# The spatial product of a gMLP block as seven products of quarters, in two passes

## The chip, the cores and the metric

One Trainium2 chip, one core. The time is device microseconds of one execution, the median of the runs; smaller is better. Next to the runs there is one execution under the hardware profiler, whose trace gives all durations used here.

## The reference

An attention block and a gMLP block follow each other on x of 2048 x 512, each after a LayerNorm. The change lies in the second:

```
h   = x + attention(layernorm(x))            # 32 heads of 16
z   = gelu(layernorm(h) @ w_in)              # 2048 x 1376, split into z1 and z of 688 columns each
z2  = layernorm(z[:, 688:])
g   = w_sp @ z2 + b_sp[:, None]              # w_sp is 2048 x 2048
out = h + (z1 * g) @ w_out                   # w_out is 688 x 512
```

## The kernel before

A row block is 128 rows, so there are 16. Matrix products are made in fp32r from two parts of each operand: a high part, rounded by a copy (ScalarE or GpSimd), and a low part, the difference (VectorE or GpSimd). `split` (line 73) makes both; `mm3` (83) issues three matmuls, high x high, high x low and low x high, into one PSUM bank.

The program has four stages: projections (243 to 527), attention (575 to 702), the z stage (719 to 769) and the gate stage (772 to 835). In the first two the order on TensorE, ScalarE, VectorE and the SP queue is written out by hand (`manual_schedule`); in the last two a scheduler orders each engine's instructions by its own estimate of times. Every engine executes its list strictly in order, and so does a DMA queue: SP issues all DMAs of these stages, in the order of its list, each after its waits.

In the z stage `load_o` (542 on) fetches a row block of the attention's output and the reciprocals of the softmax sums, and GpSimd multiplies them; `split_o` makes the parts. `make_h` (560 on) is the output projection (12 matmuls of 512 columns), the residual and the LayerNorm `hn`, whose mean, reciprocal root (`rstd_of`, ten small VectorE operations) and scaling (573) are VectorE's. `turn` (724) transposes `hn` into the parts `hT`. `make_z` (733) multiplies by w_in (48 matmuls of 344 columns), takes gelu on ScalarE, stores z1 to DRAM by SP's queue, normalises z2 on VectorE (752) and keeps both parts of it in SBUF for all 16 blocks; GpSimd makes the low part. Blocks go from 0 to 15. In one turn of the loop stand the projection of block sb+2, the transposes of sb+1 and the z matmuls of sb. The first two `make_h` lie in the last units of the attention stage. The last `invert` (620) of the attention stage takes the reciprocal of the softmax sums, which come by a DMA; its VectorE operation (624) falls into the beginning of the z stage.

In the gate stage `load_ws` (709) fetches one row block of w_sp (transposed on input, 1 MB) and splits it, one block ahead. `gate` (789) makes two PSUM banks of 344 columns, 16 x 3 matmuls each, adds the bias and multiplies by z1 on VectorE (803). `finish` (807), one block behind, transposes the product (six pieces in one PSUM tile, `pr` into `pT`), multiplies it by w_out (18 matmuls of 512 columns), adds h and stores. `load_wu` splits w_out on GpSimd.

Of the kernel before, what the change touches and what calls it, by code (L numbers as in the profile page):

```python
# [18 lines left out]
P = 128  # L19
# [5 lines left out]
EPS = 1e-5  # L25
GUESS = float(0x5F3759DF - (1 << 22) - (1 << 31))
NB = S // P
NQ = S // 512
DB = D // P
HG = H // 4  # L30
# [13 lines left out]
def block_kernel(ctx: ExitStack, tc: tile.TileContext, x, wqkv, wo, w_in, w_sp4, b_sp, w_out, out):  # L44
# [26 lines left out]
    z_scr = dram.tile([S, FH], F32, name="z_scr")  # L71

    def split(hi, lo, src, eh=None, el=None):

# [452 lines left out]
        m = LEAD  # L527


    wc = ctx.enter_context(tc.tile_pool(name="wc", bufs=3))  # L530
    early = ctx.enter_context(ExitStack())
    ec = early.enter_context(tc.tile_pool(name="early_c", bufs=1))
    e2 = early.enter_context(tc.tile_pool(name="early_2", bufs=2))
    wo2 = [wc.tile([P, DB, D], F32R, name=f"wo{i}", tag="w8") for i in range(2)]
# [24 lines left out]
    def make_h(sb, acc):  # L559
# [12 lines left out]
        hns[sb] = e2.tile([P, D], F32, name="hn")  # L572
        nc.vector.tensor_scalar(hns[sb], h, mv[:, 0:1], rs, op0=ALU.subtract, op1=ALU.mult)

    with ExitStack() as at:
        kpool1 = at.enter_context(tc.tile_pool(name="kpool1", bufs=1))
# [51 lines left out]

        def load_weights(i):

            t = wc.tile([P, DB * D], F32, name="wg", tag="w8")
# [14 lines left out]
        with tc.manual_schedule(engines={E.PE, E.Activation, E.DVE, E.SP}):  # L646
            for n in range(0, len(units), 2):
# [43 lines left out]
                if n % 32 == 16 and n < 6 * 32:  # L691
                    load_weights(n // 32)
                if n in (498, 502, 506):
                    load_o((n - 498) // 4)
                if n in (502, 506):
                    split_o((n - 502) // 4)
                if n in (504, 508):
                    make_h((n - 504) // 4, later[0].tile([P, 512], F32, name="h"))
# [7 lines left out]
    z2 = [zc.tile([P, NB, FH], F32R, name=f"z2{i}") for i in range(2)]  # L706
    wsp = [wc]

    def load_ws(tb):
        pool = wsp[tb % 2]  # L710
        t = pool.tile([P, NB, P], F32, name="wt", tag="w8")
        nc.sync.dma_start(t, w_sp4[tb])
        ws = [pool.tile([P, NB, P], F32R, name=f"ws{i}", tag="w8") for i in range(2)]
        for k in range(2):
            b = slice(k * NB // 2, (k + 1) * NB // 2)
            split(ws[0][:, b, :], ws[1][:, b, :], t[:, b, :], "act")
        return ws

    with ExitStack() as mid:
        m2 = mid.enter_context(tc.tile_pool(name="mid_2", bufs=2))  # L720
        ps = mid.enter_context(tc.tile_pool(name="mid_ps", bufs=5, space=PSUM))
        pt = mid.enter_context(tc.tile_pool(name="mid_pt", bufs=2, space=PSUM))

# [8 lines left out]

        def make_z(sb):
            hT = hTs.pop(sb)
            z = [m2.tile([P, FH], F32, name=f"z{i}") for i in range(2)]
            st = m2.tile([P, 2, 6], F32, name="zst")
            for i in (1, 0):
                for c in range(2):
# [17 lines left out]
        turn(0)  # L756
        split_o(2)
        for sb in range(NB):
            if sb + 2 < NB:
                make_h(sb + 2, ps.tile([P, 512], F32, name="acc"))  # L760
            if sb + 3 < NB:
                load_o(sb + 3)
                split_o(sb + 3)
            if sb + 1 < NB:
                turn(sb + 1)
            if sb == NB - 2:
                ws = load_ws(0)
            make_z(sb)
    early.close()


    with ExitStack() as fin:
        fc_ = fin.enter_context(tc.tile_pool(name="fin_c", bufs=1))
        f2 = fin.enter_context(tc.tile_pool(name="fin_2", bufs=2))
        wsp.append(fin.enter_context(tc.tile_pool(name="fin_w", bufs=3)))
# [3 lines left out]
        wu = [fc_.tile([P, len(FB), D], F32R, name=f"wu{i}") for i in range(2)]  # L779

        def load_wu():
            t = f2.tile([P, len(FB), D], F32, name="wg", bufs=1)
            nb, fn = len(FB) - 1, FB[-1][1]
            nc.sync.dma_start(t[:, :nb, :], w_out[:nb * P, :].rearrange("(a p) c -> p a c", p=P))
            nc.sync.dma_start(t[:fn, nb, :], w_out[nb * P:, :])
            for i, (_, n) in enumerate(FB):
                split(wu[0][:n, i, :], wu[1][:n, i, :], t[:n, i, :], "pool", "pool")

        def gate(tb, ws):

            rows = slice(tb * P, (tb + 1) * P)
            z1 = f2.tile([P, FH], F32, name="z1")
            nc.sync.dma_start(z1, z_scr[rows, :])
            g = [ps_g.tile([P, 512], F32, name="g") for i in range(2)]
            for i in range(2):
                f = slice(i * FC, (i + 1) * FC)
                for sb in range(NB):
                    mm3(g[i][:, :FC], ws[0][:, sb, :], ws[1][:, sb, :],
                        z2[0][:, sb, f], z2[1][:, sb, f], sb == 0, sb == NB - 1)
            pr = f2.tile([P, FH], F32, name="pr")  # L800
            for i in range(2):
                f = slice(i * FC, (i + 1) * FC)
                nc.vector.scalar_tensor_tensor(pr[:, f], g[i][:, :FC], bias[:, tb:tb + 1], z1[:, f],  # L803
                                               op0=ALU.add, op1=ALU.mult)
            return pr

        def finish(tb, pr):
            rows = slice(tb * P, (tb + 1) * P)
            h = f2.tile([P, D], F32, name="h")
            nc.sync.dma_start(h, h_scr[rows, :])  # L810
            pT = [f2.tile([P, len(FB), P], F32R, name=f"pT{i}") for i in range(2)]
            tp = ps_t.tile([P, 8, P], F32, name="tp")
            for i, (f0, fn) in enumerate(FB):
                nc.tensor.transpose(tp[:fn, i, :], pr[:, f0:f0 + fn], ident)  # L814
                if i in (1, 4, 5):
                    b = slice({1: 0, 4: 2, 5: 5}[i], i + 1)
                    split(pT[0][:fn, b, :], pT[1][:fn, b, :], tp[:fn, b, :], "act")
            acc = ps_o.tile([P, 512], F32, name="acc")
            for i, (f0, fn) in enumerate(FB):
                mm3(acc, pT[0][:fn, i, :], pT[1][:fn, i, :],  # L820
                    wu[0][:fn, i, :], wu[1][:fn, i, :], i == 0, i == len(FB) - 1)
            y = f2.tile([P, D], F32, name="y")
            nc.vector.tensor_add(y, acc, h)
            nc.sync.dma_start(out[rows, :], y)

        prev = None
        for tb in range(NB):
            nxt = load_ws(tb + 1) if tb + 1 < NB else None
            if tb == 0:
                load_wu()  # L830
            pr = gate(tb, ws)
            if prev is not None:
                finish(tb - 1, prev)
            prev, ws = pr, nxt
        finish(NB - 1, prev)


# [27 lines left out]
```

## Time and profile before

| | us |
|---|---|
| median of 3 runs (1926.92 to 1932.78) | 1927.6 |
| the profiled execution | 1930.47 |
| its span (first to last instruction) | 1928.7 |
| projections, attention: 0 to 1421.58 | 1421.6 |
| z stage: 1421.58 to 1594.68 | 173.1 |
| gate stage: 1594.68 to the end | 334.0 |

| engine | busy us | share of the span |
|---|---|---|
| TensorE (PE) | 1911.9 | 99% |
| VectorE (DVE) | 1444.7 | 75% |
| ScalarE (ACT) | 1261.6 | 65% |
| GpSimd (POOL) | 139.7 | 7% |

The mean granted TensorE clock is 0.998 of full speed. A row of a group gives its line, engine, operation, tiles, shapes and count, then busy time in us and mean duration in ns, then the idle time of the engine just before such instructions and what ended it. A line of the time line gives start and duration in us, the instruction, and in brackets the idle time before it and its releaser. Matmuls overlap in the array: the duration is the latency of one, and the distance between two starts is what it costs.

### The profile page before, as it was taken

The page shows a single profiled execution, that of the slowest core. Times are in us where ns is not written, and L with a number is a line of the kernel's source. Part 1 is how long each engine was busy: PE and PEld are TensorE (multiplying, and loading weights), DVE is VectorE, ACT ScalarE, POOL GpSimd, SP SyncE. Part 2 cuts the span into 40 slices and gives each one's busy share as a digit, 9 for nine tenths or more (in the row PEclk, how much of TensorE's full clock was granted, in tenths as well). Part 3 has the DMA queues.
Part 4 walks back from the last instruction along what each step waited for, and adds up shares of the span by engine and source line. Part 5 has one row for each costly group of instructions (what it writes and reads, how often), then busy time and mean ns, then how long its engine had stood idle before and what let it go on. Part 6 is the DMA issues. An engine that isn't in the chain of part 4 may idle for free.

```text
span 1928.7 us, 31977 instructions
## 1 busy us (share of the span) xinstructions
PE 1911.9 (99%) x11800; PEld 1094.2 (57%) x11800; DVE 1444.7 (75%) x2886; ACT 1261.6 (65%) x1590; POOL 139.7 (7%) x201
## 2 busy tenths in 40 slices
PE   9999999999999999999999999999999999999999
PEld 6765444444444344444444444444369999989987
DVE  6487999999999999999999999999358773232231
ACT  3335888888888888888888888888943331111110
POOL 2130000101011000000000000000012222000000
PEclk9999999999999999999999999999999999999999
DMA  5777111211221120111021021000143334232210
GB/s 187 194 190 175 40 24 32 71 24 28 50 53 49 38 40 22 31 37 24 24 53 24 13 51 37 13 13 6 29 118 118 109 119 175 81 109 92 81 66 34
DMA packets 121845, 128.90 MB, mean 67 GB/s; under 512 B 60248, under 2 KB 80744, under 8 KB 118104
## 3 DMA queue, kind: packets, MB, share of 16 engines
q1 hardware_dynamic: 121656, 126.84, 24.4%
q8 instruction: 93, 1.52, 0.3%
q14 instruction: 64, 0.52, 0.1%
q0 software_dynamic: 32, 0.01, 0.0%
HBM read 84.32 MB, written 41.55 MB: 65 GB/s over the span
## 4 chain that ended last, share of the span: by engine, by line
PE 93%; DVE 2%; DMA 1%; ACT 1%; SPq 1%; issue 1%; POOL 0%; ACTq 0%; POOLq 0%; DVEq 0%
PE pv L604 25%; PE m L200 25%; PE s L593 12%; PE acc L84 6%; PE acc L86 5%; PE acc L85 5%; PE g L85 4%; PE g L84 4%; PE g L86 4%; PE tp L814 1%; ACT pt L596 0%; DMA rc<-r_scr 0%; DVE rs_t L101 0%; DMA xr<-in_x 0%; SPq L547 0%
## 5 line engine op out<-in xcount | busy, mean ns | idle before, releaser
L596 ACT ACTIVATE pt<-s 128x1024 f32<-128x1024 f32 x1024 | 993.2, 1030 | 144.5 <-PE s L593 140.5
L205 DVE TENSOR_REDUCE mx<-m 128x1 f32<-128x512 f32 x1511 | 958.7, 684 | 105.2 <-PE m L200 64.7
L200 PE MATMUL m<-kst,qst 48*128 48x512 f32 x1511 | 607.1, 448 | 0.0
L604 PE MATMUL pv<-pt,vst 128*32 128x512 f32 x4096 | 550.7, 605 | 0.4 <-ACT o L611 0.4
L593 PE MATMUL s<-qst,kst 50*128 50x512 f32 x2048 | 465.6, 428 | 2.6 <-ACT pt L596 2.0
L200 PEld LDWEIGHTS m<-kst,qst 48*128 48x128 f32 x1511 | 263.2, 184 | 315.8 <-DVE mx L205 221.7
L593 PEld LDWEIGHTS s<-qst,kst 50*128 50x128 f32 x2048 | 223.2, 185 | 56.8 <-ACT pt L596 32.4
L200 PE MATMUL m<-uvs,qst 48*128 48x512 f32 x503 | 249.0, 496 | 0.0
L200 PEld LDWEIGHTS m<-uvs,qst 48*128 48x128 f32 x503 | 91.8, 183 | 207.3 <-DVE mx L205 205.3
L214 DVE CUSTOM_DVE_ANT_0 ab<-m,ab 128x512 f32<-128x512 f32 x252 | 171.6, 681 | 3.7 <-ACT ab L210 2.0
L604 PEld LDWEIGHTS pv<-pt,vst 128*32 128x32 f32 x4096 | 82.9, 108 | 160.9 <-issue 155.1
L76 ACT ACTIVATE ws<-wt 128x1024 fp32r<-128x1024 f32 x32 | 33.6, 1055 | 210.8 <-PE g L85 203.6
L84 PE MATMUL g<-z,ws 128*128 128x344 f32 x512 | 165.2, 323 | 0.6 <-issue 0.6
L85 PE MATMUL g<-z,ws 128*128 128x344 f32 x512 | 164.7, 322 | 0.0
L86 PE MATMUL g<-z,ws 128*128 128x344 f32 x512 | 163.4, 319 | 0.0
L210 ACT ACTIVATE ab<-m 128x512 f32<-128x512 f32 x251 | 151.0, 602 | 16.7 <-PE m L200 16.3
L803 DVE SCALAR_TENSOR_TENSOR pr<-g,bias,z 128x344 f32<-128x344 f32 x32 | 18.4, 576 | 182.3 <-PE g L86 180.3
L85 PEld LDWEIGHTS g<-z,ws 128*128 128x128 f32 x512 | 96.2, 188 | 5.8 <-issue 5.2
L84 PEld LDWEIGHTS g<-z,ws 128*128 128x128 f32 x512 | 96.2, 188 | 0.9 <-issue 0.9
L86 PEld LDWEIGHTS g<-z,ws 128*128 128x128 f32 x512 | 96.2, 188 | 0.6
L84 PE MATMUL acc<-wi,hT 128*128 128x344 f32 x256 | 83.7, 327 | 0.0
L86 PE MATMUL acc<-wi,hT 128*128 128x344 f32 x256 | 82.4, 322 | 0.0
(136 smaller groups left out, 1603.7 us busy)
## 6 DMA issues: line engine op xcount, KB each, us to landing
wt<-in_w_sp SPq DMA_DIRECT2D x16, 1024.0 KB
qst<-q_scr SPq DMA_DIRECT2D x192, 64.0 KB
kst<-k_scr SPq DMA_DIRECT2D x48, 256.0 KB
k_scr<-part SPq DMA_DIRECT2D x16, 512.0 KB
q_scr<-part SPq DMA_DIRECT2D x16, 512.0 KB
z_scr<-z SPq DMA_DIRECT2D x16, 344.0 KB
z<-z_scr SPq DMA_DIRECT2D x16, 344.0 KB
xg<-in_x SPq DMA_DIRECT2D x16, 256.0 KB
```

The costliest lines, as they stand in the source:

```text
L76: nc.scalar.activation(hi, src, AF.Copy)
L84: nc.tensor.matmul(ps, lh, rh, start=first, stop=False)
L85: nc.tensor.matmul(ps, lh, rl, start=False, stop=False)
L86: nc.tensor.matmul(ps, ll, rh, start=False, stop=last)
L200: nc.tensor.matmul(acc, q[r, p, c], keys[r, p], start=True, stop=True)
L205: nc.vector.reduce_max(at(t, e if t else e - 1), acc, axis=AX.X)
L210: nc.scalar.activation(ab[0], acc, AF.Abs)
L214: nc.vector.tensor_tensor_reduce(ab[0], acc, ab[0], 0.5, LOW, ALU.add, ALU.max, at(0, 0))
L593: nc.tensor.matmul(s[:, t, :], k[r, p, kb * P:(kb + 1) * P], q[r, p, :], start=True, stop=True)
L596: nc.scalar.activation(t, s, AF.Exp, scale=DH ** -0.5)
L604: nc.tensor.matmul(pv[0][32 * j:32 * j + 32, :], vst[hg % 2][:, c:c + 32], pts[j % 2][:, j // 2, :], start=kb == 0, stop=kb == NB - 1)
L814: nc.tensor.transpose(tp[:fn, i, :], pr[:, f0:f0 + fn], ident)
```

## The change

The four quarters of w_sp (A11 to A22, 1024 x 1024) and of z2 (B11 to B22, 1024 x 344) give the four quarters of the result by seven products, one eighth of the matmuls less, with sums of quarters ahead of and behind the products. HB is 8; p numbers a pair of row blocks, p and p+8.

- z stage: z rows run in the order 0, 8, 1, 9, ...; h rows in 0, 1, 8, 9, 2, 10, .... Both normalisations are made by ScalarE from a factor and an offset (`normal`), except for the two h in the attention stage. z1 and the normalised z2 are stored by ScalarE's queue. After each second block GpSimd makes four sums of that pair's quarters and both parts of each (`T`); for the last pair VectorE and ScalarE do.
- Pass 1 (scheduled): for each p four products, with A11-A21, (A21+A22)-A11, A22 and A21+A22 as left operands, made by VectorE from halves of rows loaded by SP (256 KB each). The second sum is stored in `s_scr`; three partial results go to `g_scr`. B11 is loaded back and split, one block per p. In the last p the loads for pass 2 (B22, B21, w_out) begin, in the buffers that pass 1 frees.
- Pass 2 (`manual_schedule` for TensorE, ScalarE and VectorE): for each p the products A11 x B11, S4 x B22, A12 x B21, the multiplication by z1 (mostly GpSimd) and the output of both row blocks, with the transposes of one block between the halves of a product.

```diff
+    z_rows = [sb + HB * i for sb in range(HB) for i in range(2)]
+    h_rows = [0, 1, HB, HB + 1] + z_rows[4:]
...
+    def normal(out, z, mv, rs, pool):
+
+        nb = pool.tile([P, 1], F32, name="nb")
+        nc.vector.tensor_scalar(nb, rs, mv[:, 0:1], -1.0, op0=ALU.mult, op1=ALU.mult)
+        nc.scalar.activation(out, z, AF.Identity, bias=nb, scale=rs)
...
+    def rows_of_a(p, e):
...
+        load_a(a11, 0, 0, p)
+        load_a(a21, 1, 0, p)
+        load_a(a22, 1, 1, p)
+        combine(e, s3, a11, a21, ALU.subtract)
+        combine(e, a21, a21, a22, ALU.add)
+        combine(e, a11, a21, a11, ALU.subtract)
+        for n in range(2):
+            nc.sync.dma_start(cut(s_scr[p])[n], a11[n])
+        return {"s3": s3, "s2": a11, "a22": a22, "s1": a21}
...
-            nc.sync.dma_start(z_scr[sb * P:(sb + 1) * P, :], z[0])
+            nc.scalar.dma_start(z_scr[0][rows, :], z[0])
...
-            rs = rstd_of(m2, mv[:, 1:2], 1)
-            nc.vector.tensor_scalar(z[1], z[1], mv[:, 0:1], rs, op0=ALU.subtract, op1=ALU.mult)
-            split(z2[0][:, sb, :], z2[1][:, sb, :], z[1],
-                  "act" if sb < NB - 1 else None, "pool" if sb < NB - 2 else None)
+            normal(z[1], z[1], mv, rstd_of(m2, mv[:, 1:2], 1), m2)
+            nc.scalar.dma_start(z_scr[1][rows, :], z[1])
...
+            e = nc.gpsimd if el else nc.vector
...
+            e.tensor_sub(b11, b12, b11)
+            e.tensor_sub(b12, b22, b12)
+            e.tensor_sub(t2, b22, b11)
+            put_t("t3", b12)
+            put_t("t2", t2)
+            put_t("t1", b11)
+            e.tensor_sub(b11, b21, t2)
+            put_t("n4", b11)
...
+        for k in range(NB):
+            if k + 2 < NB:
+                make_h(h_rows[k + 2], ps.tile([P, 512], F32, name="acc"))
...
+            if k + 1 < NB:
+                turn(z_rows[k + 1])
+            make_z(z_rows[k])
+            if k == NB - 2:
+                raw = rows_of_a(0, nc.vector)
+                ops = {n: put(w[i], raw[n]) for i, n in enumerate(("s3", "s2", "a22"))}
...
+        for p in range(HB):
...
+            load_b(b11, 0, 0, p)
+            if p:
+                product(g7, ops["s3"], T["t3"])
+            else:
+                for blocks in (range(HB - 1), range(HB - 1, HB)):
+                    product(g7, ops["s3"], T["t3"], blocks)
+                    product(g6, ops["s2"], T["t2"], blocks)
...
+                b22 = [zc.tile([P, HB, FC], F32R, name="b22", tag=f"t3_{i}") for i in range(2)]
+                for k in range(HB):
+                    load_b(b22, 1, 1, k)
...
+            nc.scalar.activation(p6, g6, AF.Copy)
+            nc.vector.tensor_add(p67, g7, p6)
...
+            product(g4, ops["a22"], T["n4"])
+            keep(1, g4, p67)
...
+            product(g5, ops["s1"], T["t1"])
+            keep(2, g5, p67)
+            keep(0, g5, p6)
...
+                product(g1, a11, b11, halves[0])
+                if prev:
+                    prev.turn((0, 2), (2, 5), (5, 6))
+                product(g1, a11, b11, halves[1])
...
+                (nc.gpsimd if p else nc.vector).tensor_mul(bot.pr, bot.pr, z1[1])
...
+                if prev:
+                    prev.multiply(range(len(FB)))
+                product(g3, s4, b22, halves[0])
...
+                bot.turn((0, 2), (2, 5), (5, 6))
+                product(g3, s4, b22, halves[1])
+                nc.vector.tensor_add(right, g3, right)
+                nc.gpsimd.tensor_mul(right, right, z1[0][:, FC:])
...
+                bot.multiply(range(len(FB)))
+                product(g2, a12, b21, halves[0])
+                bot.store()
...
+                product(g2, a12, b21, halves[1])
+                nc.vector.tensor_add(left, g2, left)
+                (nc.vector if last else nc.gpsimd).tensor_mul(left, left, z1[0][:, :FC])
```

More of the change, by code (lines that the diff above doesn't have):

```diff
@@ new lines, in load_a, with cut, put, combine @@
+    def load_a(halves, i, j, p):
+        for n, t in enumerate(halves):
+            nc.sync.dma_start(t, w_sp4[p + HB * i][:, HB * j + QB * n:HB * j + QB * n + QB, :])
+    def cut(t):
+        return [t[:, QB * n:QB * n + QB, :] for n in range(2)]
+    def put(slot, halves):
+        op = slot.take()
+        for n in range(2):
+            parts(cut(op[0])[n], cut(op[1])[n], halves[n])
+        return op
+    def combine(e, out, a, b, op):
+        for n in range(2):
+            e.tensor_tensor(out[n], a[n], b[n], op)
@@ L756, in block_kernel @@
[L756 to L768, printed above, removed]
+            normal(z[1], z[1], mv, rstd_of(m2, mv[:, 1:2], 1), m2)
+            nc.scalar.dma_start(z_scr[1][rows, :], z[1])
@@ L789, in gate @@
[L789 to L794, printed above, removed]
-            for i in range(2):
[L796 to L835, printed above, removed]
+        b11 = [bc.tile([P, HB, FC], F32R, name=f"b11_{i}") for i in range(2)]
+        def load_b(b, i, j, k):
+            t = f1.tile([P, FC], F32, name="b", bufs=3)
+            nc.sync.dma_start(t, z_scr[1][(HB * i + k) * P:(HB * i + k + 1) * P, j * FC:(j + 1) * FC])
+            parts(b[0][:, k, :], b[1][:, k, :], t)
@@ new lines, in product, with load_wu @@
+        def product(acc, a, b, blocks=range(HB)):
+            for k in blocks:
+                mm3(acc, a[0][:, k, :], a[1][:, k, :], b[0][:, k, :], b[1][:, k, :],
+                    k == 0, k == HB - 1)
+        def load_wu(i, hi, lo):
+            f0, fn = FB[i]
+            t = e2.tile([P, D], F32, name="wu", tag="hn", bufs=3)
+            nc.sync.dma_start(t[:fn], w_out[f0:f0 + fn, :])
+            parts(hi, lo, t[:fn], "pool")
+        f = [Slot(fs, f"f{i}") for i in range(3)]
+        ops["s1"] = put(f[0], raw["s1"])
@@ new lines, in block_kernel, with __init__, turn, multiply @@
+        class Out:
+            def __init__(self, tb, h, pr):
+                self.rows, self.h, self.pr = slice(tb * P, (tb + 1) * P), h, pr
+                self.pT = self.acc = None
+            def turn(self, *groups):
+                if self.pT is None:
+                    self.pT = [f2.tile([P, len(FB), P], F32R, name=f"pT{i}") for i in range(2)]
+                    self.tp = ps_t.tile([P, 8, P], F32, name="tp")
+                for i0, i1 in groups:
+                    fn = FB[i1 - 1][1]
+                    for i in range(i0, i1):
+                        f0, n = FB[i]
+                        nc.tensor.transpose(self.tp[:n, i, :], self.pr[:, f0:f0 + n], ident)
+                    split(self.pT[0][:fn, i0:i1, :], self.pT[1][:fn, i0:i1, :],
+                          self.tp[:fn, i0:i1, :], "act")
+            def multiply(self, blocks, end=True):
+                first = self.acc is None
+                if first:
+                    self.acc = ps_o.tile([P, 512], F32, name="acc")
+                for i in blocks:
+                    n = FB[i][1]
+                    mm3(self.acc, self.pT[0][:n, i, :], self.pT[1][:n, i, :], wu[0][i], wu[1][i],
+                        first and i == blocks[0], end and i == blocks[-1])
+            def store(self):
+                y = f2.tile([P, D], F32, name="y")
+                nc.vector.tensor_add(y, self.acc, self.h)
+                nc.sync.dma_start(out[self.rows, :], y)
```

187 lines of the change are left out of this document (153 added, 34 removed).

## The prediction

> **What bounds the kernel now.** I read the busy time by stage first, then the matmul pitch in the time line of the last stage, then what TensorE waited for around the two stage borders, and last the costs of the engines that get new work. Busy time by stage (columns: window, length, busy time of each engine with its instructions, granted clock, DMA share, GB/s); the two lines are the z stage (lines 719 to 768) and the gate stage (772 to 835):
>
> ```profile
> core 0: us, PE busy (x) PEld busy (x) DVE busy (x) ACT busy (x) POOL busy (x), PEclk, DMA share, GB/s
> 1421.58:1594.68 173.10, 169.26 (x1003) 159.93 (x1001) 134.44 (x395) 57.66 (x112) 39.48 (x26) 0.99 0.38 115
> 1594.68:1928.70 334.02, 329.17 (x1920) 300.33 (x1920) 87.19 (x128) 47.04 (x78) 12.89 (x12) 1.00 0.27 92
> ```
>
> TensorE fills both. In the gate stage VectorE is busy 26% of the time and ScalarE 14%, so matmuls taken out there are time taken out until another resource is full. The time line gives what one costs, and the groups by line what follows it:
>
> ```profile
> 1644.27 0.32 PE L85 MATMUL g<-z,ws 128*128 128x344 f32 x1
> ...
> 1645.36 0.32 PE L86 MATMUL g<-z,ws 128*128 128x344 f32 x1
> ...
> L803 DVE SCALAR_TENSOR_TENSOR pr<-g,bias,z 128x344 f32<-128x344 f32 x32 | 18.4, 576 | 182.3 <-PE g L86 180.3
> ```
>
> The starts run from 1644.27 to 1645.36 in seven steps: 0.156 us per 344-column matmul (0.32 is its latency). A row block takes 20.57 us (chain: 1632.45 to 1653.05, 20.60), of which 96 x 0.156 = 15.0 is the gate and 5.57 the transposes and 18 output matmuls (pitch 0.233, 4.2 us).
>
> **What goes.** A pair of row blocks (p, p+8) had 2 x 96 = 192 gate matmuls; seven quarter products of 8 blocks x 3 are 168. So 24 x 0.156 = 3.74 us per pair, times 8: 30.0 us. The written order also sets each block's transposes in one run between two half products, where 1645.5 to 1653.0 now changes six times between transposes, output and gate matmuls. 5.57 us hold 4.2 of output matmuls and 0.8 of six transposes (four take 0.57 in the z stage); of the 0.57 left I take 0.13 a block off, 2 us in all (bounds 0 and 9). Gain 32 us, if the products are fed.
>
> **What the feeding costs in the steady blocks.** Pass 1, 15.0 us of TensorE per p. VectorE: 6 sums and 8 low parts of 128x512 at half of the 1.2 us that a 128x1024 subtraction takes alone (1626.05), 14 x 0.61 = 8.5, four adds out of PSUM at about 0.5 (three products are kept and p67), a low part of B11 0.45: 11 us, 73%. ScalarE: 8 copies of 128x512 at 0.62 and two of 344 at 0.46, 5.9 us. Both are under 15, and the operands of p+1 are made during p, six slots for four operands, so nothing of it is late. Pass 2, 22 us per p: 3 x 0.58, 8 x 0.61, six pT low parts 2.5, two y 1.4, two adds 1.0: 11.5 us on VectorE. The one short path is g2 to the next p's transposes: add 0.5, GpSimd's multiply (688 columns take 1.74, so 344 take 0.87), hops 0.2: 1.6 us against a half product of 12 x 0.156 = 1.87. Bounds 0 and 0.7 us for each of seven p; I take 0.15, 1 us.
>
> The z stage keeps its matmuls. VectorE gives the two normalisations to ScalarE (0.61 and 0.79 a block) and gets two 128x1 factors (0.2 each). ScalarE gets 1.4 us and two DMA issues (0.3 to 0.7 each on SP) to about 3.4 us of 10.8. GpSimd had 1.74 + 1.29 a block:
>
> ```profile
> L81 POOL TENSOR_TENSOR z<-z,z 128x688 fp32r<-128x688 f32 x14 | 24.4, 1742 | 24.3 <-ACT z L76 22.3 <-PE acc L86 2.0
> L78 POOL CAST wqk<-wg 128x512 fp32r<-128x512 f32 x6 | 3.7, 614 | 38.9 <-DMA wg<-in_wqkv 38.9
> L81 DVE TENSOR_TENSOR o<-o,o 128x512 fp32r<-128x512 f32 x13 | 17.8, 1367 | 11.5 <-ACT o L76 11.5
> ...
> 1610.82 3.53 POOL L81 TENSOR_TENSOR wu<-wg,wu 128x512 fp32r<-128x512 f32 x2
> 1610.98 4.45 DVE L81 TENSOR_TENSOR ws<-wt,ws 128x1024 fp32r<-128x1024 f32 x2 [0.36 <-ACT ws L76]
> ```
>
> Now a pair of blocks costs it 8 sums at 0.87, 4 casts at 0.41 and 2 multiplies by 1/l at 1.29: 11.2 of 21.5 us. Its order puts the multiply two blocks ahead of use, so a nine-operation chain (7 us) before it has 12 us to spare. The last two lines show the danger: beside each other, two VectorE subtractions take 4.45 us instead of 2.36 and two of GpSimd's 3.53 instead of 2.54. In the z stage only the o subtraction has two SBUF inputs, and its mean is already 1.37 us. I take 0 for the steady z stage (bound: 1 us a block). The Trainium skill (SBUF — State Buffer, SBUF: two separate sides) says that these two engines share a port pair as an exclusive lock held for a whole instruction, against a VectorE operation with two SBUF inputs. The lines agree in kind; by that rule shorter GpSimd operations also mean shorter waits.
>
> **The four seams**, where the order has no cover:
>
> A. Start of the z stage. The z rows now run 0, 8, 1, 9, and h of row 8 is made only in the first turn. TensorE's order after the last weighing is: transposes of 0, output projection of 8, 39 z matmuls, transposes of 8. VectorE's order has the reciprocal of the softmax sums ahead of the factor that hn of 8 needs, and that reciprocal waits for a DMA:
>
> ```profile
> 1435.09 0.25 DVE L624 RECIPROCAL rc<-sums 128x16 f32<-128x16 f32 x1 [3.25 <-DMA sums<-o]
> 1435.26 0.45 DVE L573 TENSOR_SCALAR hn<-xr,mv,rs_u 128x512 f32<-128x512 f32 x1
> ...
> 1426.10 0.32 PE L84 MATMUL acc<-wi,hT 128*128 128x344 f32 x1
> ...
> 1436.42 0.60 PE L729 MATMUL tp<-ident,hn 128*128 128x128 f32 x4
> ```
>
> Before, TensorE reached the hn behind it at 1436.42, after 48 z matmuls and another projection: no wait. Now it is there at 1426.1 + 39 x 0.156 = 1432.2, while hn comes at 1435.3 + 0.2 (factor) + 0.6 (ScalarE) + hops = 1436.3: 4.1 us idle. SP's DMA order up to the sums is the same. What an idle time costs beyond itself is seen at the end of the z stage:
>
> ```profile
> PE tp L729 <- DVE hn L573: 2.0, 1, 2.0
> ...
> 1576.00:1578.00 2.00, 1.19 (x8) 1.22 (x9) 1.79 (x8) 0.52 (x1) 0.00 (x0) 0.90 0.94 324
> 1578.00:1580.00 2.00, 2.00 (x9) 2.00 (x8) 1.00 (x2) 0.85 (x2) 0.65 (x1) 0.50 0.76 284
> 1580.00:1582.00 2.00, 2.00 (x12) 2.00 (x11) 0.52 (x1) 0.46 (x1) 1.00 (x1) 0.75 0.02 7
> ```
>
> After 2 us without work the granted clock fell to 0.50 for some 3.4 us (1577.6 to 1581.0): 1.7 us more. The Trainium skill (TensorE: Matmul & The Clock Gate, What's actually happening) has the clock halve after an idle window of about 3.4 us; here 2 us sufficed. So A costs 4.1 + 1.7 = 5.8 us (bounds 1 and 8).
>
> B. That same place. Six sums and puts of w_sp now stand in VectorE's order before hn of row 15: some 10.3 us of work after the last projection, where two 1024-wide subtractions stood; but 16 z matmuls (2.5 us) now stand ahead of those transposes. About 0.6 us remains of the 2.0 and the clock drop may go: gain 1.5 (bounds: gain 3.5, loss 3).
>
> C. Start of pass 1. 42 matmuls (6.5 us) cover the last pair's sums, which take about 3.6 us after the last z matmul. Then s3 of p=1 waits for an A21 whose buffer is freed late: ready at about 14.3 us, needed at 15. I take 0.7 (0 to 4).
>
> D. Between the passes. SP's order has eight B22, eight B21, three w_out blocks and three stores, and only then q, z1 and h of the first pair. Three staging tiles serve the 16 B loads, so each load waits for a copy and a subtraction three loads earlier. Nearest rows: r_scr 2.24 us to landing, 0.62 a copy, 1.29 a GpSimd subtraction, 0.4 an issue. With 2.2 to 2.4 us a load, I get the last B21 issued 15.6 us after the last g7, q at 16, the lower z1 at 17.2. These four move 2.0 MB; at 320 GB/s (324 at 1576) z1 lands near 22.6, and 0.9 us of multiply makes it 23.5. TensorE reaches the first transposes after g6, g4, g5, g1 and half of g3: 4.5 x 3.74 = 16.9. Idle 6.6, clock 1.7: 8.3 us (bounds 1 and 13).
>
> The tail keeps its form (one pT wait, +0.5).
>
> **Sum.** -32.0 + 5.8 - 1.5 + 0.7 + 8.3 + 1.0 + 0.5 = -17.2. The profiled execution took 1930.47 us, 1928.7 of them the span, and lies 2.9 above the median of 1927.6. So 1913.3 by it, and 1910.4 against the median; I say 1911.
>
> **Rivals.**
> 1. The seams are covered: D's loads come early and the reciprocal's DMA too. For it: the scheduler placed those loads by its own times. Against it: the 3.25 us wait is in the trace. A and D at 2 each: -27, 1900. Chance 0.14.
> 2. The seams are twice my price, or pass 1 loses 1.5 us per p to waits between ScalarE and VectorE in order: +12 to +14, 1924. For it: 73% of VectorE in strict order. Chance 0.16.
> 3. Slower: the DMA engines bound both passes. Pass 1 moves 2.80 MB per p (1.5 w_sp, 0.5 s, 0.5 g, 0.18 B11, in binary units) in 15 us, 187 GB/s; pass 2 3.85 MB in 22 us, 175 GB/s; together 53.2 MB. At 160 GB/s that is 332 us where 329 stood, and with A and B the kernel takes about 1935; below some 165 GB/s it is slower than before. Against it: 188 to 193 GB/s from 0 to 145 us at a DMA share of 0.60 to 0.76, so 250 to 310 at full use. For it: none of these transfers is 1 MB any more. Chance 0.08. The Trainium skill (DMA: Bandwidth & Descriptors, Bandwidth) wants DMAs of 1 MiB or more, and its table has 138 GB/s at 64 KB and 341 at 1 MB; an estimate between them for 256 KB is 200 to 250, which would leave little spare.
>
> The rest, 0.62, is my forecast. That the change doesn't do what it says has no room: TensorE's order holds 168 gate matmuls a pair.
>
> **Numbers.** About 0.3% (5.8 us) is what a measurement of this kernel can tell from no change: faster means under 1921.8. Forecast and rival 1 are faster (0.76), rival 2 a third of the time (0.05): 0.81; the same 0.08, out of rival 2; slower 0.11, rival 3 and the far end of 2. The range reaches from rival 1 to rival 2: 1899 to 1926.
>
> **What would show it.** Right: g matmuls 1344 for 1536; pass 1 blocks near 15.0 us and pass 2 near 22; an idle of about 4 us before the second group of hn transposes and of 4 to 8 us before the first pr transposes, each followed by a clock of 0.50; DMA share near 0.65. Wrong: blocks of 17 us or more in pass 1 with TensorE waiting for ws, or z blocks longer than 10.8 us with GpSimd named.

## The result and the profile after

The changed kernel takes 1971.24 us (median of 4 runs, 1969.83 to 1973.82) against 1928.0 for the kernel before: a ratio of 1.0221 (95% interval 1.0200 to 1.0241), 43 us slower. The prediction was 1911, 17 us faster, so both the sign and the range were wrong. The profiled execution has a span of 1968.6 us, 39.9 more than before.

Busy time by stage after (columns as in the prediction: window, length, PE, PEld, DVE, ACT, POOL, granted clock, DMA share, GB/s). The lines are the z stage, pass 1, the seam between the passes, and pass 2 in three pieces:

```profile
core 0: us, PE busy (x) PEld busy (x) DVE busy (x) ACT busy (x) POOL busy (x), PEclk, DMA share, GB/s
1421.00:1595.90 174.90, 168.53 (x1008) 159.17 (x1006) 121.01 (x405) 72.19 (x131) 84.61 (x96) 1.00 0.53 162
1595.90:1715.90 120.00, 119.93 (x765) 119.64 (x764) 86.70 (x156) 47.28 (x90) 0.00 (x0) 1.00 0.56 183
1715.90:1739.30 23.40, 5.88 (x39) 5.63 (x38) 14.49 (x19) 8.81 (x18) 8.22 (x6) 0.73 0.71 224
1739.30:1800.00 60.70, 49.49 (x231) 41.38 (x232) 26.76 (x44) 13.73 (x28) 7.70 (x6) 0.85 0.51 173
1800.00:1900.00 100.00, 84.79 (x420) 71.55 (x419) 45.16 (x73) 21.32 (x44) 12.84 (x10) 0.93 0.43 136
1900.00:1968.60 68.60, 54.46 (x277) 44.52 (x276) 24.39 (x42) 11.43 (x25) 7.38 (x6) 0.98 0.13 43
```

Pass 1 is what was forecast: its eight p take 120.8 us (from the first product at 1595.13 to the first of pass 2 at 1715.92), 15.1 each, with TensorE full and the clock at 1.00. The z stage, taken as before from the first transposes of `hn` (1421.07) to the first product behind it, takes 174.1 us, 1.0 more than before. All the rest is behind 1715.9: 252.7 us, where the prediction's terms come to 186 (eight p of 22, and 8.3 + 1.0 + 0.5). There TensorE is busy 77% of the time, and its clock is below full. The waits of TensorE name what it stood for (total us, times, longest):

```profile
PE tp L991 <- DVE pT L84: 36.1, 31, 3.5
PE tp L991 <- DMA q<-g_scr: 17.5, 1, 17.5
PE tp L791 <- ACT hn L570: 4.7, 2, 3.1
```

The third line is one wait at the start of the z stage and one in its middle:

```profile
1434.97 0.66 PE L791 MATMUL tp<-ident,hn 128*128 128x128 f32 x4 [3.06 <-ACT hn L570]
...
1538.59 0.66 PE L791 MATMUL tp<-ident,hn 128*128 128x128 f32 x4 [1.67 <-ACT hn L570]
```

The second is the seam between the passes. There SP issues the last staged load of B21 and then the first pair's partial results:

```profile
1727.57 0.32 SPq L865 DMA_DIRECT2D b<-z_scr  x1
1731.19 0.37 SPq L961 DMA_DIRECT2D q<-g_scr  x1
```

The first line is new: 31 waits, two for nearly each of the 16 blocks, before the transposes of the product. One block in the time line of TensorE, and the VectorE operations beside it:

```profile
1759.98 0.38 PE L991 MATMUL tp<-ident,pr 128*128 128x128 f32 x2
1761.37 0.55 PE L991 MATMUL tp<-ident,pr 128*128 128x128 f32 x3 [1.01 <-DVE pT L84]
1763.09 0.29 PE L991 MATMUL tp<-ident,pr 128*48 128x128 f32 x1 [1.17 <-DVE pT L84]
```

```profile
1758.96 2.02 DVE L743 TENSOR_TENSOR ws<-a,ws 128x512 fp32r<-128x512 f32 x2
1760.90 0.41 DVE L84 TENSOR_TENSOR pT<-tp,pT 128x256 fp32r<-128x256 f32 x1
1762.47 0.56 DVE L84 TENSOR_TENSOR pT<-tp,pT 128x384 fp32r<-128x384 f32 x1 [1.16 <-ACT pT L79]
```

The first low part ends at 1761.31 and the second group of transposes starts at 1761.37; the second ends at 1763.03 and the third group starts at 1763.09. All three groups write one PSUM tile `tp`; each waits until ScalarE and VectorE have read the group before it. From 1759.98 to 1763.14, when the next product matmul starts, is 3.16 us; without the waits six transposes would take about 0.6, estimated from four in the z stage (1434.97 to the next matmul at 1435.39).

The kernel before has the same tile and the same dependency, in the stretch that the prediction looked at (TensorE, then VectorE):

```profile
1645.52 0.38 PE L814 MATMUL tp<-ident,pr 128*128 128x128 f32 x2
...
1648.53 0.49 PE L814 MATMUL tp<-ident,pr 128*128 128x128 f32 x3
...
1650.25 0.27 PE L814 MATMUL tp<-ident,pr 128*48 128x128 f32 x1
```

```profile
1647.85 0.42 DVE L81 TENSOR_TENSOR pT<-tp,pT 128x256 fp32r<-128x256 f32 x1
1649.58 0.56 DVE L81 TENSOR_TENSOR pT<-tp,pT 128x384 fp32r<-128x384 f32 x1 [0.19 <-ACT pT L76]
```

There too each group starts 0.1 to 0.3 us after the low part (1648.27, 1650.14). But its scheduler had put output and gate matmuls into the gaps, and no idle time shows. What I read as switches that cost time was the cover.

The idle time brings a second loss. These stretches cover the block above and what follows it:

```profile
1760.00:1761.00 1.00, 0.36 (x3) 0.12 (x2) 1.00 (x3) 0.38 (x1) 0.00 (x0) 1.00 0.18 50
1761.00:1762.00 1.00, 0.55 (x3) 0.31 (x3) 0.31 (x1) 0.05 (x1) 0.00 (x0) 1.00 0.93 290
1762.00:1763.00 1.00, 0.00 (x0) 0.00 (x0) 0.53 (x1) 0.44 (x1) 0.00 (x0) 1.00 0.80 271
1763.00:1764.00 1.00, 0.91 (x6) 0.91 (x7) 0.31 (x2) 0.27 (x1) 0.00 (x0) 1.00 0.71 244
1764.00:1765.00 1.00, 1.00 (x6) 1.00 (x5) 0.00 (x1) 0.00 (x0) 0.00 (x0) 0.58 0.06 23
1765.00:1766.00 1.00, 1.00 (x5) 1.00 (x5) 0.00 (x0) 0.00 (x0) 0.00 (x0) 0.50 0.00 0
```

2.18 us of waiting within 2.7 us, and from about 1764.2 on TensorE is busy at half clock, a granted clock of 0.50 (until 1767.6, as the stretches behind these give it). This comes back in many blocks: the mean clock of pass 2 is 0.92.

### The profile page after: what moved, and what is told of

Read it like the earlier page. It is cut to its first block, busy times and chain, and to the rows that moved or that the text cites. A ratio compares the mean times of both kernels' runs of the same rounds, so it can differ in the third digit from the quotient of the medians.

```text
span 1968.6 us, 32474 instructions
## 1 busy us (share of the span) xinstructions
PE 1897.0 (96%) x11608; PEld 1075.5 (55%) x11608; DVE 1541.4 (78%) x3101; ACT 1331.7 (68%) x1735; POOL 207.8 (11%) x287
## 4 chain that ended last, share of the span: by engine, by line
PE 85%; DVE 6%; DMA 4%; ACT 2%; issue 1%; SPq 1%; POOL 1%; ACTq 0%; DVEq 0%; POOLq 0%
PE pv L620 25%; PE m L203 25%; PE s L609 12%; PE acc L87 6%; PE acc L88 5%; PE acc L89 5%; DVE ws L743 2%; DMA a<-in_w_sp 2%; PE g L87 2%; PE g L89 1%; PE g L88 1%; PE tp L991 1%; DVE a L762 1%; DVE pT L84 1%; DMA b<-z_scr 1%
## 5 line engine op out<-in xcount | busy, mean ns | idle before, releaser
L213 ACT ACTIVATE ab<-m 128x512 f32<-128x512 f32 x251 | 151.1, 602 | 16.7 <-PE m L203 16.3
L81 POOL CAST mparts<-nm 128x16 fp32r<-128x16 f32 x32 | 6.3, 196 | 910.1 <-DVE nm L223 910.1
L742 ACT ACTIVATE ws<-a 128x512 fp32r<-128x512 f32 x80 | 46.4, 625 | 64.7 <-PE g L89 41.9
L87 PE MATMUL acc<-wi,hT 128*128 128x344 f32 x256 | 83.0, 324 | 0.0
L88 PE MATMUL acc<-wi,hT 128*128 128x344 f32 x256 | 81.8, 319 | 0.0
L89 PE MATMUL acc<-wi,hT 128*128 128x344 f32 x256 | 81.8, 319 | 0.0
L79 ACT ACTIVATE pT<-tp 128x256 fp32r<-128x256 f32 (+2 forms) x48 | 18.3, 381 | 79.8 <-PE tp L991 79.8
L991 PE MATMUL tp<-ident,pr 128*128 128x128 f32 (+1 forms) x96 | 20.5, 296 | 53.6 <-DVE pT L84 36.1
L742 ACT ACTIVATE ws<-s 128x512 fp32r<-128x512 f32 x32 | 20.1, 631 | 74.9 <-DVE s L762 74.9
L87 PE MATMUL g<-b,ws 128*128 128x344 f32 x192 | 68.6, 358 | 0.0
L743 DVE TENSOR_TENSOR ws<-a,ws 128x512 fp32r<-128x512 f32 x80 | 56.8, 753 | 15.1 <-ACT ws L742 14.9
```

Of the source, the lines that this page charges most:

```text
L87: nc.tensor.matmul(ps, lh, rh, start=first, stop=False)
L88: nc.tensor.matmul(ps, lh, rl, start=False, stop=False)
L89: nc.tensor.matmul(ps, ll, rh, start=False, stop=last)
L213: nc.scalar.activation(ab[0], acc, AF.Abs)
L742: nc.scalar.activation(hi, src, AF.Copy)
L743: (nc.gpsimd if el == "pool" else nc.vector).tensor_sub(lo, src, hi.bitcast(F32))
```

## The experiments

Theory 1: the shared PSUM tile makes each group wait for VectorE (36 us), half clock follows (about 16 us), and at the seam the first pair's tiles lie in memory that the last readers of pass 1 hold. Theory 2: VectorE's order or the DMA rate bounds pass 2. The times are medians of 2 to 8 runs. The experiments were measured in three groups, each with the kernel before beside it (1930.96, 1930.55 and 1930.9 us); ratios are to those.

**Spread order.** The groups are set apart in the written order; nothing else is changed.

```diff
-product(g1, a11, b11, halves[0])
-if prev: prev.turn((0, 2), (2, 5), (5, 6))
-product(g1, a11, b11, halves[1])
+product(g1, a11, b11, range(4))
+if prev: prev.turn((0, 2))
+product(g1, a11, b11, range(4, 7))
+if prev: prev.turn((2, 5))
+product(g1, a11, b11, range(7, 8))
...
-if prev: prev.multiply(range(len(FB)))
+if prev:
+    prev.multiply(range(3), False)
+    prev.turn((5, 6))
...
+    prev.multiply(range(3, 6))
```

The same for `bot` in the second product.

> Only the written order of pass 2 is changed: the three groups of transposes of a block stand apart (after blocks 0 to 3 of a product, after 4 to 6, and after the first three of the six output blocks) instead of in one run. Theory 1 (the groups share one PSUM tile, so each waits for VectorE's low part of the group before it: 31 waits, 36.1 us, and the clock drops that follow): these waits fall below 6 us, the mean clock of pass 2 rises from 0.94 to 0.98 or more, the period of a p falls from 27 to 23 us: 1926 to 1936 us. Theory 2 (pass 2 is bound by VectorE's strict order or by the DMA rate): the idle time moves to products that wait for operands (g waiting for b21, s4 or z1), 1958 or more. Theory 3 (the clock falls for another reason than these waits): the waits go and the clock stays at 0.94, about 1941.

Measured: 1919.88 us, ratio 0.9946 (0.9923 to 0.9968). This order alone is worth 51 us against after (49 between the profiled executions), more than I had expected, and the kernel is then 11.1 us, 0.5%, faster than before. TensorE's waits, and a stretch of pass 2:

```profile
PE tp L991 <- DVE pr L1030: 18.3, 1, 18.3
PE tp L791 <- ACT hn L570: 4.6, 2, 3.2
PE tp L991 <- DVE pT L84: 3.1, 2, 2.1
```

```profile
1760.00:1905.00 145.00, 145.00 (x794) 124.28 (x793) 76.06 (x137) 38.56 (x84) 23.77 (x20) 1.00 0.47 146
```

The 36.1 us have become 3.1; TensorE does not pause for 145 us and its clock is 1.00. From one bottom block's first transposes to the next (1766.45, 1788.22, 1810.03) is 21.8 us, where it was 28.7 (1759.98 to 1932.18 in six). From 1740 to the end (after, then this run):

```profile
1740.00:1968.60 228.60, 188.15 (x922) 157.26 (x922) 96.31 (x158) 46.47 (x97) 27.93 (x22) 0.92 0.36 118
1740.00:1919.40 179.40, 171.80 (x922) 146.47 (x920) 87.99 (x158) 45.14 (x97) 25.63 (x22) 0.98 0.47 151
```

For the same 922 records TensorE is busy 16.3 us less: that is half clock that is gone. With the 33.0 of waits it is 49.3; the spans differ by 49.2. Theories 2 and 3 fall. What is left is the seam.

**A tile for each group.** The order of after, but each group takes a PSUM tile of one bank, two in turn.

```diff
-                    self.tp = ps_t.tile([P, 8, P], F32, name="tp")
                 for i0, i1 in groups:
+                    self.tp = ps_t.tile([P, 4, P], F32, name="tp", tag=f"tp{0 < i0 < 5:d}")
```

> The order of after is kept; each group of transposes gets a PSUM tile of one bank of its own, two tiles in turn, so the second group waits for nobody and the third only for the reader of the first. Theory 1: of 2.2 us a block about 0.6 stays, so 25 of the 36.1 us go and about half of pass 2's lost clock: 1935 to 1945. Theory 2 (VectorE's order or the DMA rate bounds pass 2): 1958 or more, with the waits put elsewhere. If the cost were in the switching between transposes and matmuls, as my prediction had it: no change, 1971.

Measured: 1931.46 us (ratio 1.0004, 0.9993 to 1.0015), 40 us less than after with not one instruction moved on TensorE, and a little under the range expected.

```profile
PE tp L991 <- DVE pT L84: 12.7, 15, 3.3
```

15 waits are left, about one a block: the third group, which takes the first one's tile again. This settles that the cost is the tile and not the switching between transposes and products. The Trainium skill (PSUM — Partial Sum Buffer, PSUM bank collisions raise a hardware error) says that a TensorE write and a read by another engine may not meet in one bank and quadrant, whatever the columns, and that software has to guard by bank. By it the waits of after could not have been left out: blocks 0 to 3 of `tp` fill one 2 KB bank, 4 and 5 lie in the next, so the second group shares a bank with the first and the third with the second. No run here shows a collision; that separate tiles of one bank each take the wait away is what this run shows. It changes tile and bank together, so it does not tell which of the two the second group had waited for.

**No written order in pass 2.**

```diff
-        with tc.manual_schedule(engines={E.PE, E.Activation, E.DVE}):
+        with ExitStack():
```

> Pass 2's written order is taken away: the scheduler orders TensorE, ScalarE and VectorE there, as it does in the gate stage of before. Theory 1: it places matmuls between the groups of transposes, as it did before, so most of the 36.1 us go; 1925 to 1950. Theory 2 (the resources bound pass 2, not the order): 1960 or more. If it starts other work too early for the first pair's loads, the 17.5 us grow.

Measured: 1913.71 us, ratio 0.9911 (0.9882 to 0.9940). The scheduler again places matmuls between the groups and, for the first pair, more products ahead of them: no group of transposes in pass 2 is listed as waiting for a low part, and the wait at the seam is 7.6 us:

```profile
PE tp L991 <- DMA q<-g_scr: 7.6, 1, 7.6
```

Against after, the written order costs 57 us, more than I had expected.

**The seam: early loads and six staging tiles.**

```diff
+            if last:
+                qz = zc.tile([P, HB * FC], F32, name="qz", tag="t1_1")
+                ...  # q and z1 of the first pair into qz, behind g5
...
-            t = f1.tile([P, FC], F32, name="b", bufs=3)
+            t = f1.tile([P, FC], F32, name="b", bufs=6)
```

> The first pair's partial results and z1 are loaded early, in the memory of an operand that the last p of pass 1 has done with, and the loads of B22 and B21 go through six staging tiles instead of three; pass 2's order is that of after. Theory 1 (the 17.5 us before the first pr transposes come from the chain of staged B loads, behind which these four loads stand, and from memory that pass 1's last readers hold): the wait falls to 2 to 6 us and the clock of 0.50 behind it goes: 1950 to 1960. Rival (the 17.5 us are DMA rate: the same bytes have to come first): under 4 us of it go, 1966 or more.

Measured: 1973.85 us: a miss, nothing gained. From the waits of this run at 1690 to 1780:

```profile
PE tp L1004 <- DVE pT L84: 12.2, 6, 6.7
...
PE tp L1004 <- DVE pr L1040: 9.0, 1, 9.0
...
DVE pr L1038 <- DMA g_scr<-q: 7.7, 1, 7.7
```

and ScalarE's time line:

```profile
1740.21 1.34 ACT L742 ACTIVATE ws<-a 128x512 fp32r<-128x512 f32 x2 [5.18 <-DMA a<-in_w_sp]
1741.45 0.37 ACT L79 ACTIVATE pT<-tp 128x256 fp32r<-128x256 f32 x1
```

The first wait is shorter by 8.5 us, but VectorE's first write to the product tile waits 7.7 us for pass 1's stores of its partial results, whose memory that tile takes. Then the second group waits 6.7: ScalarE's order has the next pair's A11 ahead of the first copy out of PSUM, and stood 5.18 us for its load. Behind 1740 the 922 matmul records take 194.57 us, 6.4 more than in after, at a mean clock of 0.90 (0.92 in after).

**B21 behind the first pair's loads** (with the spread order).

```diff
-                for k in range(HB):
-                    load_b(b21, 1, 0, k)
...
         prev, nxt = None, fetch(0)
+        bs = zc.tile([P, HB, FC], F32, name="bs", tag="t1_1")
+        ...  # two DMAs; the parts are made after turn((2, 5)) and turn((5, 6)) of the first p
```

> On top of the spread order of pass 2: the eight staged loads of B21 leave the last p of pass 1; B21 comes in two DMAs behind the first pair's loads, and its parts are made in the first p of pass 2 behind the second and third group of transposes. Theory 1 (the 18.3 us before the first pr transposes are the chain of staged B21 loads: the first pair's tiles lie in memory that the chain's last subtraction, at 1731.2, sets free): the first pair's partial results are issued near 1724 instead of 1731.8, the wait falls to 6 to 11 us, the half clock behind it shrinks; 1906 to 1913 against 1919.9. Rival (w_out's blocks or the three stores of partial results hold that memory as long, or DMA rate sets the landing): the wait stays at 15 us or more, 1916 to 1921.

Measured: 1919.07 us (0.9936, 0.9914 to 0.9959) against 1919.88: within the rival's range, and no gain. SP, VectorE and GpSimd at the seam, a row of each:

```profile
1731.23 0.37 SPq L959 DMA_DIRECT2D q<-g_scr  x1
```

```profile
1735.52 1.54 DVE L1036 SCALAR_TENSOR_TENSOR pr<-g,bias,q 128x344 f32<-128x344 f32 x3 [13.90 <-DMA z<-z_scr]
```

```profile
1728.34 1.26 POOL L743 TENSOR_TENSOR wu<-wu,wu 48x512 fp32r<-48x512 f32 x1
```

VectorE is done with pass 1 at 1721.6, ten us earlier, and then stands idle 13.9; the first pair's load is still issued at 1731.23. GpSimd works on w_out until 1729.6, and the stores, issued up to 1726.5, are on their way; SP's wait before that load is put down to them (4.0 us). So the B21 chain was not alone in holding this load. Whether it waits for the memory of the stored tiles, or for `g_scr`, which it reads and they write, this run does not tell.

**The seam and the start of the z stage** (on top of that: h rows in the order of the z rows from the start, one more buffer for z's second half, A11's parts behind the bottom block's transposes).

```diff
-    h_rows = [0, 1, HB, HB + 1] + z_rows[4:]
+    z_rows[1:3] = [1, HB]
+    h_rows = z_rows
```

> Spread order and late B21 as in the run beside it; besides, the early h rows are 0 and 8 (then in the order of the z rows), so that the second group of hn transposes does not wait for the reciprocal of the softmax sums, and in pass 2 the parts of the next A11 stand behind the bottom block's transposes in ScalarE's order, not ahead of them. Theory 1: the 3.1 us at the start of the z stage go, with the clock drop that followed it in some runs (mean clock 0.98 to 1421-1500); the first pT no longer waits for the next pair's A11 (2 to 3 us at the first p). 1900 to 1907. If the idle at the start of the z stage only moves to the end of that stage (VectorE is as late there): no gain from it, 1905 to 1910.

Measured: 1915.72 us, ratio 0.9924 (0.9901 to 0.9948): 3.4 us below its base, which is less than the 5.8 us that the prediction takes as the least that can be told from no change, and above both ranges expected. The first wait at the seam is 14.5 us (15.2 in its base).

**The row order**, on after (with the same extra buffer for z):

> After with one edit: the early h rows are 0 and 8 and all h rows follow the z rows' order (each z row has its hn two turns ahead). Theory 1 (the wait of 3.06 us at 1434.97 is the reciprocal behind a DMA, ahead of the factor for hn of row 8): that wait goes, 1966 to 1969. Rival (VectorE is as far behind at the end of the z stage, so the idle time comes back there): 1970 to 1973.

Measured: 1980.38 us (ratio 1.0249, 1.0220 to 1.0279; after 1.0221), a miss, 9 us above after. The wait of 3.1 us is gone, but there are now five of up to 1.7 us:

```profile
PE tp L792 <- ACT hn L571: 3.5, 5, 1.7
```

4.7 before, 3.5 now: the idle time moved. The first product of pass 1 starts at 1597.38, where it was 1595.13, and 1.6 us of that is a longer wait in the projections (2.2 us at line 321, 0.6 in after), which the edit does not touch. The other 7 us lie in pass 2, which the edit does not touch either: the pT waits are 36.6 there, but the mean clock is 0.89 against 0.92. Why the clock was lower there was not tested.

**The parts of z2's sums by ScalarE and VectorE**, on after:

```diff
-    put_t = lambda n, t: parts(T[n][0][:, k, :], T[n][1][:, k, :], t, el, el)
+    put_t = lambda n, t: parts(T[n][0][:, k, :], T[n][1][:, k, :], t)
```

> After with one edit: both parts of the sums of z2 are made by ScalarE (high) and VectorE (low) instead of GpSimd; GpSimd keeps the sums. My reading: GpSimd's part costs the z stage nothing (174.9 us after, 173.1 before, of which 3.1 are the wait at its start), so the stage stays at 174 to 176 and the time at 1969 to 1974. Rival (GpSimd's longer chain or its use of memory ports beside VectorE slows the z stage): the stage falls to 171 to 172, 1967 to 1969. Other rival (VectorE has no room for four more subtractions a pair): 178 or more, 1974 to 1980.

Measured: 1990.02 us, ratio 1.0299 (1.0269 to 1.0329), 19 us above after: the third case, and by more than I gave it. Pass 1 begins at 1610.73, 15.6 us later.

```profile
PE tp L791 <- ACT hn L570: 13.8, 7, 3.5
```

hn's chain on VectorE and ScalarE is now what TensorE waits for: 9.1 us more than in after. In the z stage TensorE is also busy 4.6 us longer (173.10 us, 168.53 in after), at a mean clock of 0.98. So GpSimd's share saves some 16 us.

**z stored by SP's queue**, with the spread order:

```diff
-            nc.scalar.dma_start(z_scr[0][rows, :], z[0])
+            nc.sync.dma_start(z_scr[0][rows, :], z[0])
```

(and the same for `z_scr[1]`).

> On top of e1 (spread order): z1 and the normalised z2 are stored by SP's queue, as z1 was in the kernel before, not by ScalarE's. My reading (0 in the sum): ScalarE has room, its DMA issues cost the stage nothing, and SP's queue has room too: z stage 174 to 176, 1918 to 1922. Rival (two issues of 0.3 to 0.7 us a block hold ScalarE's gelu chain): the z stage loses 1 to 3 us, 1916 to 1918. Other rival (on SP the stores wait for the normalisation and hold the loads of o, x and w_sp behind them): 1924 or more.

Measured: 1940.02 us (1.0050, 1.0034 to 1.0066), 20 us above the spread order. Pass 1 begins at 1617.26 instead of 1594.26. In the z stage (ScalarE's and SP's waits):

```profile
ACT z L807 <- DMA z_scr<-z: 38.1, 9, 7.1
```

```profile
SPq L554 <- POOL o L558: 59.1, 10, 8.0
```

SP stands in its order for GpSimd to free the buffers of o, the stores of z queue behind that, and gelu waits for the buffer of the store. TensorE waits 9.6 us for hn (4.6 in the spread order) and 8.5 us for gelu to empty its banks. So the third case again, with the blame the other way round: the loads hold the stores.

**First pair's memory set apart** (on top of the run with the late B21 and the new row order).

```diff
+                qz = zc.tile([P, HB * FC], F32, name="qz", tag="t1_1")
+                qt = zc.tile([P, HB * FC], F32, name="qt", tag="t1_0")
+                ...  # q, z1 and both products of the first pair in these; B21 through eight separate places
...
-            parts(hi, lo, t[:fn], "pool")
+            parts(hi, lo, t[:fn])
```

> On top of e17 (spread order, late B21): the first pair's partial results, its z1 and its product tiles lie in the memory of operands that g5, the last product of pass 1, has done with, so that none of them waits for the other readers of pass 1's pools; w_out's low parts are VectorE's, not GpSimd's. Theory 1 (the 14.5 us left before the first pr transposes are memory: the late B21 run stayed at 15.2 because GpSimd's w_out subtractions, up to 1729.6, and the three stores held the same memory): these loads are issued near 1717, the first transposes come near 1726, and the wait falls to 3 to 7 us, with less of the half clock: 1902 to 1909 against 1915.7. Rival (the bytes set the time: DMA share is 0.86 at 1716 to 1740 in e17, and these loads go beside others): the wait stays above 10 us, 1912 or more.

> e19 without the written order of pass 2: the scheduler orders TensorE, ScalarE and VectorE. It took 5.4 us off the time against the spread order before (1913.7 against 1919.1 to 1919.9), by more products ahead of the first transposes. If the seam is still open in e19, this is 2 to 5 us faster than e19; if it is closed there, within 2 us of it: 1898 to 1909.

Measured: 1917.82 us (0.9937, 0.9922 to 0.9952) with the written order and 1910.65 us (0.9901, 0.9883 to 0.9919) without it, both above what I expected. TensorE's waits in the first:

```profile
PE g L87 <- ACT b L743: 5.7, 1, 5.7
PE tp L1006 <- DVE qt L1055: 5.2, 1, 5.2
```

The wait for the first pair falls from 14.5 to 5.2 us. That memory was part of it is argued from here and from the run with early loads, where the first write to `pr`, which reads nothing that is stored, waited 7.7 us for the stores. This run does not show it by itself: the loads also stand further ahead in SP's order, and w_out's low parts moved from GpSimd to VectorE. The time does not follow, since the third product now waits 5.7 us for B21, whose last two staged loads are issued at 1739.95, behind the next pair's, and half clock follows (0.83 from 1740 to 1760, against 1.00 in its base). Between 1716 and 1760 the DMA engines move 253 to 257 GB/s at a share of 0.78 to 0.79. How much of the rest of the seam is that rate, and how much the order of the queue, was not separated. The scheduler's order hides 7 us more of it, more than the 2 to 5 expected. That version, 1910.65 against 1930.9, is the fastest of all here.

## Why the prediction was wrong, point by point

- **What goes (30.0): right.** 15.1 us per p in pass 1, and 21.8 in pass 2 once TensorE is fed (forecast 22): 36.9 for a pair that took 41.2. That is 4.3 less, 3.74 of it the 24 matmuls; what gives the other 0.6 was not tested.
- **Transposes in one run (a gain of 2): the step that failed.** It had the wrong sign. The 0.57 us left of the 5.57 behind each gate was read as the price of switching. But the switches (nine from 1645.36 to 1652.98, not six) were how the scheduler had laid matmuls over two evacuations of `tp`. Writing the groups one behind the other uncovered them: 36.1 us of waits and 16.3 of half clock. The bounds (0 and 9) did not go below nothing, and no rival named the tile: I had costed the VectorE and ScalarE work of a turn, not asked which matmuls stood between a group and the next write to its tile.
- **Steady pass 1: right**, VectorE 72% (73 forecast). **The slower rival (DMA rate): wrong**; pass 1 ran at 183 GB/s and share 0.56 with TensorE full. The Trainium skill (DMA: Bandwidth & Descriptors, Bandwidth) wants DMAs of 1 MiB or more; pass 1 of this trace, with 172 and 256 KB, did not stand for any of its loads. And from 1741 to 1749 DMAs of 256 to 516 KB moved 405 GB/s, well above the 200 to 250 that the prediction estimated for 256 KB.
- **z stage at no cost: nearly right**; one wait of 1.7 us came in its middle (1538.59). Either part done the other way costs 16 to 23 us there.
- **A (5.8): 3.1 measured**, and no half clock behind it in the profiled run (1.00 to 1595.9). **B (-1.5): more than forecast.** TensorE does not wait before the last transposes of hn (1581.36), so both the 2.0 us and the clock drop of 1.7 are gone. These three give the stage's difference: 3.1 + 1.7 - 3.7 is about 1.0. **C (0.7): nothing.** No wait for s3 of p = 1 came; the 0.6 us of idle time ahead of the first product stood before the gate stage too (0.59).
- **D (8.3, bounds 1 and 13): mis-sized.** TensorE arrives as forecast (the last g7 ends at 1704.6, and 16.9 on is 1721.5; 1721.7 measured), but waits 17.5 us where 6.6 were forecast. The clock is then 0.50 until 1750.5; TensorE works 6.6 of these 11.3 us, so this costs 3.3 more, and D is 20.8, outside its bounds. The last B21 load was set 15.6 us after that g7, at 1720.2, by counting staged loads; it came at 1727.57. The first pair's load was to follow 0.4 us later and followed after 3.6, at 1731.19. The first 7.4 us are the staged chain itself, whose low parts on VectorE took 0.52 us by their median and up to 1.48. In the other 3.2 SP still waited for that chain; the run without it shows that other holders end as late. The clock term (1.7) was taken from a 2 us idle and does not hold for 17.5.
- **The seven steady p of pass 2 (1.0): right** in the spread order, where they have no wait to speak of.
- **Rival 2 (the seams at twice my price): half true.** A to D were 13.3 in the sum and came to 20.2 (3.1 - 3.7 + 0 + 20.8), and pass 1 lost nothing to waits.

The terms as measured add up: eight pairs at 4.3 less (-34.4), 1.0 in the z stage, 20.8 in D and 52.4 for the failed step come to about 40, and the spans differ by 39.9.

Without the failed step the time would have come out inside the range in spite of D: the spread order is 11.1 us faster than before and the scheduler's order, which also hides more of the seam, 17.2, where 17 were forecast. That these two figures meet is luck: the scheduler's order is not the one that was forecast, and several terms were off in opposite directions.

## What to carry to other kernels

Where an operation on the bounding engine leaves a result in PSUM that others have to read, ask what runs between it and the next write to the same tile; a scheduler may have been hiding that wait, and a written order has to keep the matmuls in between or give each group a bank. A gap beside a wait that shows no idle time is cover, not cost. And where a new pool takes over memory, its first loads and writes can wait for the last reader of what lay there, on any engine or in a store, and not only for the queue ahead of them; ask for each of them who that reader is.

## What the runs showed of the hardware that was not expected

Half clock needs no long pause: two waits of 1.01 and 1.17 us, 0.6 apart with three transposes between, were followed by 3.4 us at half clock, while 3.06 us at one go (1431.9 to 1435.0 in after) were followed by none. The Trainium skill (TensorE: Matmul & The Clock Gate, What's actually happening) has the clock halve after an idle window of about 3.4 us; the first case differs from that, the second does not. After the long idle at the seam the return to full clock came 11.3 us after TensorE went on in after and 9.3 in the spread order; waits fell into both, and TensorE worked 6.6 and 7.3 us of it. The clock had fallen 4.9 and 3.8 us after TensorE stopped.

VectorE and GpSimd beside each other were slower again: at the seam of the spread order two low parts of 128x344, 0.52 us each alone, took 2.88 us beside GpSimd's subtractions for w_out:

```profile
1718.58 0.52 DVE L743 TENSOR_TENSOR b<-b,b 128x344 fp32r<-128x344 f32 x1 [0.34 <-ACT b L742]
1719.48 2.88 DVE L743 TENSOR_TENSOR b<-b,b 128x344 fp32r<-128x344 f32 x2 [0.38 <-ACT b L742]
```

```profile
1719.20 4.29 POOL L743 TENSOR_TENSOR wu<-wu 128x512 fp32r<-128x512 f32 x3 [128.46 <-DVE b L743]
```
